# Block attention and a gated feed-forward on one core: first q by hardware queues, earlier data moves, a limit of three loads in flight, and new instruction orders

## The chip, the cores and the metric

The kernel runs on one core of one Trainium2 chip. The metric is device microseconds of one execution. "Span" is the length of the profiled execution on the core; the times stand about 1.8 us above it. Most executions of the kernel before lie within 0.5% of their median. A run more than 1.5% above the fastest of its kernel is called slow and is left out of ratios, but medians are of all runs. Where a profile is quoted it is of a fast run, unless the text says otherwise.

Engines as the profile names them: PE (TensorE matmuls), PEld (TensorE weight loads), DVE (VectorE), ACT (ScalarE), POOL (GpSimd), SP (SyncE); a q behind the name is that engine's queue or sequencer.

## The reference

```python
# q, k, v: (8 batches, 8 heads, 576 positions, 64), blocks of 64 positions
scores = q_block @ k_block.T / 8
attn   = exp(scores - max) / (sum + 1e-9)
x      = attn @ v_block                # 4608 tokens x 512 after the transpose of heads
h      = ((x @ w1) * (x @ w2)) @ w3    # d_ff = 1024
out    = h @ w_out                     # 4608 x 512
```

## The kernel before

The tokens are cut into 18 "pairs" of 256 tokens; two pairs are a group, which from pair 4 on shares one run through w1 and w2. w3 and w_out are multiplied once into one matrix (steps V, W, Z), so that each pair needs only one output product (O). A string gives the program order of all steps; each engine runs its own instructions in that order.

```python
# letter = step, number = pair; a few lines of the order
q0.0 k0.0 q0.1 k0.1 v0 q1.0 q1.1 k1.0 k1.1 i0 v1 q2 k2 i1 v2 i2 i3 q3 k3 v3 o h0 h1 q4 k4 v4
D0.0.32.64 T0.0.0 T0.1.0 T0.0.1 S0.0 T0.1.1 q5 k5 v5 E0.0 S0.1 E0.1 P0.0 P0.1 ...
# q k v i o h  loads by GpSimd, cast from f32 to bf16 on the way (i = quarter of w1 and w2)
# T  transpose of q or k on VectorE, in 32x32 blocks      S  scores   E  exp on ScalarE
# P  attention times v   N  normalise   X  transpose of x on VectorE
# G  SyncE moves of q and k, H  SyncE moves of x: from pair 8 on, into rows that allow 64x64 matmuls
# A B  x times w1, x times w2 into the halves of one PSUM tile
# C  copy of half A to SBUF (ScalarE)   M  C's copy times half B (VectorE)
# O Y Q  output product, copy, store   D  warm-up matmuls on zeros
# in profiles: s_ps is the PSUM tile of S, pv of P, ab_ps of A and B, w_ps of W, o_ps of O; a_sb is C's copy

def load(dst, src):
    return inorder(nc.gpsimd.dma_start(dst, src))

def do_P(p, hh=None):                   # ... cut
    if p < 8:      # 32-row blocks: 64 small matmuls a pair
        ...
    else:          # moved data: 32 matmuls of 64x64
        for g, r in ((0, 0), (1, 1), (1, 0), (0, 1)):
            mm(pv[half[g], r, m * W:(m + 1) * W], lhsT=e[half[r], u, 4 * g + m, :],
               rhs=vbuf[p % 6][half[r], u, 4 * g + m, 0:W], start=True, stop=True)

def do_C(p, j):
    a_t[p, j] = msb.tile([P, 512], f32, tag="a_sb", bufs=3, name="a_sb")
    inorder(nc.scalar.copy(a_t[p, j][:], ps_t[p, j][:, 0, :]))
```

q and k share five buffers, v has six: a load also waits until its buffer has been read.

The softmax here doesn't subtract the row's maximum and nothing guards it: scores larger than these inputs give would overflow.

Of the kernel before, what the change touches and what calls it, by code (L numbers as in the profile page):

```python
# [9 lines left out]
q0.0 k0.0 q0.1 k0.1 v0 q1.0 q1.1 k1.0 k1.1 i0 v1 q2 k2 i1 v2 i2 i3 q3 k3 v3 o h0 h1 q4 k4 v4  # L10
D0.0.32.64 T0.0.0 T0.1.0 T0.0.1 S0.0 T0.1.1 q5 k5 v5 E0.0 S0.1 E0.1 P0.0 P0.1 T1.0.0 N0.0 T1.1.0
T1.0.1 S1.0 T1.1.1 q6 k6 v6 E1.0 X0.0 S1.1 N0.1 X0.1 P1.0 E1.1 T2.0 A0.0 T2.1 q7 k7 B0.0 C0.0 P1.1
v7 M0.0 A0.1 N1.0 B0.1 C0.1 X1.0 S2 N1.1 E2 M0.1 X1.1 P2 A1.0 N2.0 B1.0 X2.0 C1.0 A1.1 N2.1 B1.1
M1.0 C1.1 X2.1 A2.0 M1.1 B2.0 C2.0 A2.1 M2.0 B2.1 T3.0 C2.1 A0.2 M2.1 B0.2 C0.2 T3.1 q8 k8 v8 A1.2
M0.2 B1.2 C1.2 S3 M1.2 A2.2 E3 B2.2 C2.2 P3 M2.2 A0.3 N3.0 B0.3 X3.0 C0.3 A1.3 N3.1 B1.3 M0.3 C1.3
X3.1 A2.3 M1.3 B2.3 C2.3 A3.0 M2.3 B3.0 V0 C3.0 A3.1 M3.0 B3.1 V1 C3.1 A3.2 M3.1 B3.2 C3.2 V2 A3.3
M3.2 B3.3 C3.3 V3 W0 M3.3 T4.0 W1 Z0 V4 V5 T4.1 q9 k9 v9 W2 Z1 V6 V7 T5.0 S4 Z2 W3 T5.1 q10 k10 E4
T6.0 T6.1 P4 v10 q11 k11 Z3 S5 N4.0 O0 E5 X4.0 N4.1 X4.1 T7.0 O1 T7.1 Y0 Q0 T8.0 P5 v11 q12 k12 Y1
S6 T8.1 O2 Q1 E6 N5.0 X5.0 N5.1 X5.1 O3 T9.0 T9.1 Y2 G4.0 P6 v12 q13 k13 A4.0 N6.0 B4.0 G4.1 Y3 X6.0
N6.1 C4.0 A4.1 X6.1 B4.1 C4.1 M4.0 Q2 S7 Q3 M4.1 A4.2 E7 T10.0 B4.2 C4.2 T10.1 P7 v13 q14 k14 A4.3  # L20
M4.2 B4.3 N7.0 C4.3 A4.4 X7.0 M4.3 B4.4 C4.4 N7.1 A4.5 M4.4 B4.5 C4.5 X7.1 S8 M4.5 S9 E8 A4.6 T11.0
# [23 lines left out]
def kernel(  # L45
# [11 lines left out]
    nc = tc.nc  # L57
    B, H, S, D = q.shape
# [36 lines left out]
    def load(dst, src):  # L95
        return inorder(nc.gpsimd.dma_start(dst, src))  # L96
# [14 lines left out]
    vbuf = [consts.tile([P, 2, H, VW], bf, name=f"vbuf{i}") for i in range(6)]  # L111
# [16 lines left out]
    HH = H // 2  # L128

# [51 lines left out]
    def do_G(g, a):  # L181
# [250 lines left out]
```

## Time and profile before

Time 251.4 us (median of 4 runs, 249.8 to 252.8); span 249.3 us.

| engine | busy us | share of the span |
|---|---|---|
| TensorE matmuls | 226.9 | 91% |
| VectorE | 154.5 | 62% |
| ScalarE | 83.4 | 33% |
| GpSimd (issuing loads) | 86.9 | 35% |

The prediction shows the lines that carry the reading. In the rows of digits there the span is cut into 40 equal slices, and each digit is the busy share of one in tenths (9 is 90% or more); in the row PEclk it is the TensorE clock that was granted. From the list of waits (engine, line, what it waited for, then total us, times, longest us): VectorE's transposes of q and k waited for q loads three times in all.

```profile
DVE qkT L177 <- DMA qk<-in_q_dram: 8.3, 3, 3.1
```

All three of those waits end by 20.2 us, and those for k by 22.4. After that the loads were always ahead of the transposes.

### The profile page before, as it was taken

The numbers are of one execution on the slowest core, as the hardware profiler recorded it, in microseconds if no ns is written. First come the engines' busy times: TensorE is split into PE (matmuls) and PEld (weight loads), VectorE is DVE, ScalarE is ACT, GpSimd is POOL, SyncE is SP. The second block draws the span as 40 slices with busy tenths as digits, with TensorE's granted clock in tenths as the row PEclk, the third lists the DMA queues.
The fourth block names the chain that finished last, engine by engine and source line by source line (L and its number), as shares of the span: only waits on it lengthen the run. The fifth ranks groups of instructions, "written<-read, shape, count | busy, mean of one in ns | idle before, by whom it ended". The sixth has DMA issues, their size and how long they took to land.

```text
span 249.3 us, 6372 instructions
## 1 busy us (share of the span) xinstructions
PE 226.9 (91%) x2740; PEld 122.0 (49%) x2760; DVE 154.5 (62%) x236; ACT 83.4 (33%) x116; POOL 86.9 (35%) x116
## 2 busy tenths in 40 slices
PE   3328899999999999999999999999999999999992
PEld 2225688874455445444444444444444444444441
DVE  2566965899879588999998798918440331233000
ACT  2110324332343333535335325262332332331322
POOL 8977854486997254573660000000000000000000
PEclk9999999999999999999999999999999999999998
DMA  7999999999999999999999974635502200400334
GB/s 67 145 165 182 193 185 201 196 174 172 155 169 209 221 225 249 177 209 193 204 194 235 271 128 99 147 76 199 151 3 84 84 0 9 162 0 1 139 116 168
DMA packets 93660, 37.12 MB, mean 149 GB/s; under 512 B 77120, under 2 KB 86592, under 8 KB 93632
## 3 DMA queue, kind: packets, MB, share of 16 engines
q0 software_dynamic: 84736, 19.41, 84.6%
q1 hardware_dynamic: 8896, 17.31, 24.0%
q8 instruction: 22, 0.36, 0.6%
q14 instruction: 6, 0.05, 0.1%
HBM read 38.80 MB, written 9.44 MB: 194 GB/s over the span
## 4 chain that ended last, share of the span: by engine, by line
PE 73%; DMA 17%; POOL 3%; DVE 2%; issue 1%; ACT 1%; SPq 0%; DVEq 0%; ACTq 0%; POOLq 0%
PE ab_ps L93 41%; PE o_ps L93 22%; DMA out_dram<-o_sb 6%; DMA w<-in_moe_w_dram 6%; PE w_ps L93 6%; DMA qkm<-qkT 5%; PE s_ps L93 3%; PE pv L93 2%; POOL qk L96 2%; DVE qkT L177 1%; POOL vbuf L96 1%; ACT e L209 0%; DVE ab L321 0%; POOL w L96 0%; ACT a_sb L306 0%
## 5 line engine op out<-in xcount | busy, mean ns | idle before, releaser
L93 PE MATMUL ab_ps<-xt,w 128*128 128x512 bf16 (+1 forms) x697 | 130.0, 343 | 1.1 <-DMA w<-in_moe_w_dram 0.5
L93 PEld LDWEIGHTS <-w 128*128 128x128 bf16 x704 | 67.8, 99 | 55.6 <-DMA w<-in_moe_w_dram 0.9
L321 DVE TENSOR_TENSOR ab<-a_sb,ab_ps 128x512 bf16<-128x512 f32 x72 | 48.9, 679 | 49.3 <-ACT a_sb L306 49.2
L306 ACT COPY a_sb<-ab_ps 128x512 f32<-128x512 f32 x72 | 42.2, 585 | 87.9 <-PE ab_ps L93 85.9
L93 PE MATMUL o_ps<-w3o,ab 128*128 128x512 bf16 (+1 forms) x285 | 63.3, 373 | 0.6
L177 DVE STREAM_TRANSPOSE qkT<-qk 128x1024 bf16<-128x1024 bf16 (+1 forms) x40 | 45.6, 1178 | 11.0 <-DMA qk<-in_q_dram 8.3
L93 PEld LDWEIGHTS <-ab 128*128 128x128 bf16 x296 | 28.5, 98 | 32.2
L96 POOL DMA_DIRECT2D vbuf<-in_v_dram x40 | 33.8, 854 | 14.6 <-DMA qk<-in_q_dram 6.4
L351 ACT COPY o_sb<-o_ps 128x1024 f32<-128x1024 f32 x17 | 17.2, 1012 | 42.8 <-PE o_ps L93 38.8
L239 DVE TENSOR_TENSOR xn<-pv,rc 128x512 bf16<-128x512 f32 x36 | 24.9, 692 | 1.2
L96 POOL DMA_DIRECT2D qk<-in_k_dram x26 | 20.2, 782 | 10.0 <-DMA vbuf<-in_v_dram 7.3
L96 POOL DMA_DIRECT2D qk<-in_q_dram x26 | 20.3, 788 | 8.2 <-DMA qk<-in_k_dram 2.3
L209 ACT ACTIVATE e<-s_ps 128x1024 bf16<-128x1024 f32 (+1 forms) x18 | 17.1, 978 | 8.9 <-PE s_ps L93 8.7
L93 PE MATMUL pv<-vbuf,e 64*32 64x65 bf16 (+1 forms) x832 | 11.0, 200 | 4.5 <-DMA vbuf<-in_v_dram 3.3
L93 PE MATMUL w_ps<-wo,w3T 128*128 128x512 bf16 x62 | 14.0, 379 | 0.1
L93 PEld LDWEIGHTS <-e 64*32 64x32 bf16 (+1 forms) x832 | 8.3, 99 | 11.5 <-issue 6.6
L236 DVE RECIPROCAL rc<-pv 128x8 f32<-128x8 f32 x36 | 6.9, 192 | 11.3 <-PE pv L93 11.2
L96 POOL DMA_DIRECT2D w<-in_moe_w_dram x16 | 11.1, 696 | 7.4 <-DMA wo<-in_moe_w_out_dram 3.4
L259 DVE STREAM_TRANSPOSE xm<-xn 128x512 bf16<-128x512 bf16 x20 | 13.6, 697 | 0.2
L251 DVE STREAM_TRANSPOSE xt<-xn 128x512 bf16<-128x512 bf16 x16 | 11.3, 707 | 0.4
L93 PEld LDWEIGHTS <-qkT 32*64 32x64 bf16 x512 | 5.8, 116 | 11.2 <-DVE qkT L177 9.2
L344 DVE COPY o_sb<-o_ps 128x256 f32<-128x256 f32 x1 | 0.4, 424 | 16.0 <-PE o_ps L93 16.0
(19 smaller groups left out, 45.4 us busy)
## 6 DMA issues: line engine op xcount, KB each, us to landing
out_dram<-o_sb SPq DMA_DIRECT2D x17, 512.0 KB, 2.9
qkm<-qkT SPq DMA_DIRECT2D x40, 128.0 KB, 7.2
vbuf<-in_v_dram POOLq DMA_DIRECT2D x32, 128.0 KB, 8.7
w<-in_moe_w_dram POOLq DMA_DIRECT2D x16, 256.0 KB, 10.0
qk<-in_q_dram POOLq DMA_DIRECT2D x10, 256.0 KB, 8.3
qk<-in_k_dram POOLq DMA_DIRECT2D x10, 256.0 KB, 10.1
xt<-xm SPq DMA_DIRECT2D x40, 64.0 KB, 3.0
qk<-in_q_dram POOLq DMA_DIRECT2D x8, 128.0 KB, 5.1
```

The source lines that it names most:

```text
L93: return inorder(nc.tensor.matmul(*a, **kw))
L96: return inorder(nc.gpsimd.dma_start(dst, src))
L177: inorder(nc.vector.transpose(qkT_t[g][:, :, p % 2, s, heads(h)].rearrange("p e h (y t) -> p h t e y", t=2), qk_t[p][:, s, heads(h)].rearr ...
L209: inorder(nc.scalar.activation(e_t[p][:, :, heads(hh)], s_t[p][:].rearrange("p u (h q) -> p u h q", q=CH)[:, :, heads(hh)], Exp, scale=sca ...
L236: inorder(nc.vector.reciprocal(rc[:], pv[:, :, :, D:W]))
L239: inorder(nc.vector.tensor_mul(xn_t[p][:, u], pv[:, :, :, 0:D], rc.to_broadcast([P, 2, 4, D])))
L251: inorder(nc.vector.transpose(new_xt(g)[:].rearrange("p (o t) -> p o t", o=KO)[:, :, t0:t0 + UT] .rearrange("p o (m y) -> p m o y", y=BL), ...
L259: inorder(nc.vector.transpose(xm_t[g][:, u, :, m].rearrange("p o (c y) -> p c o y", y=BL), xn_t[p][:].rearrange("p u r m d -> p (u r) m d" ...
L306: inorder(nc.scalar.copy(a_t[p, j][:], ps_t[p, j][:, 0, :]))
L321: inorder(nc.vector.tensor_mul(o, view(a_t.pop((p, j))[:]), view(ps_t.pop((p, j))[:, 1, :])))
L344: inorder(copy(o_sb[:, u, n0:n1], t[:, 0, 0:n1 - n0]))
L351: inorder(nc.scalar.copy(o_sb[:], ps_t.pop(p)[:]))
```

## The change

Its intent: start sooner, by taking the first q out of GpSimd's queue and by a better order of loads; give pairs 6 and 7 the cheaper 64x64 form of attention times v; and from pair 8 on keep the load queue short, so that the moves of q, k and x arrive sooner. The instruction orders were searched anew for all of it.

```diff
+    last = []
+    tick = consts.tile([P, 1], bf, name="tick")
-    def load(dst, src):
-        return inorder(nc.gpsimd.dma_start(dst, src))
+    def load(dst, src, paced=False):
+        if paced:                       # paced: p >= 8
+            inorder(nc.gpsimd.tensor_copy(tick[0:1], last[-3]))
+        ins = inorder(nc.gpsimd.dma_start(dst, src))
+        ...                             # last.append(one element of dst)
+        return ins
+    def do_R(h):                        # first q, half h, f32
+        raw_t[h] = msb.tile([P, HH, 2 * D], f32, tag="o_sb", name="raw")
+        inorder((nc.sync, nc.scalar)[h].dma_start(raw_t[h][:], q[0, heads(h), 0:4 * CH, :]...))
+    def do_K(h):
+        inorder(nc.scalar.copy(qk_t[0][:, 0, heads(h)], raw_t[h][:]))
     # do_P, do_X, do_AB, do_M: the moved form of x; do_G, do_H: other order of the moves (below)
-    if p < 8:
+    if p < 6:
-    vbuf ... range(6)     ab ... bufs=3
+    vbuf ... range(7)     ab ... bufs=4
 ORDER
-q0.0 k0.0 q0.1 k0.1 v0 q1.0 q1.1 k1.0 k1.1 i0 v1 q2 k2 i1 v2 i2 i3 q3 k3 v3 o h0 h1 q4 k4 v4
+R0 R1 k0 v0 q1 k1 v1 i1 i0 q2 k2 v2 i2 i3 q3 k3 v3 h0 o h1 q4 k4 v4 K0 K1 T0.0 T0.1 q5 k5 v5 S0 E0
 ...                                    # nearly all of the rest is new too
```

The one-element copy reads what the load three back has written. GpSimd therefore stands still until that load has landed: at most three loads are in flight.

Two things are cut from the diff. do_D makes its warm-up matmuls in another form. do_G and do_H issue their moves in another order, and the first four moves of x of a group now need only the first transpose of each of its pairs; before, each four needed both.

More of the change, by code (lines that the diff above doesn't have):

```diff
@@ L9 @@
 ORDER = """
-q0.0 k0.0 q0.1 k0.1 v0 q1.0 q1.1 k1.0 k1.1 i0 v1 q2 k2 i1 v2 i2 i3 q3 k3 v3 o h0 h1 q4 k4 v4
-D0.0.32.64 T0.0.0 T0.1.0 T0.0.1 S0.0 T0.1.1 q5 k5 v5 E0.0 S0.1 E0.1 P0.0 P0.1 T1.0.0 N0.0 T1.1.0
-T1.0.1 S1.0 T1.1.1 q6 k6 v6 E1.0 X0.0 S1.1 N0.1 X0.1 P1.0 E1.1 T2.0 A0.0 T2.1 q7 k7 B0.0 C0.0 P1.1
-v7 M0.0 A0.1 N1.0 B0.1 C0.1 X1.0 S2 N1.1 E2 M0.1 X1.1 P2 A1.0 N2.0 B1.0 X2.0 C1.0 A1.1 N2.1 B1.1
-M1.0 C1.1 X2.1 A2.0 M1.1 B2.0 C2.0 A2.1 M2.0 B2.1 T3.0 C2.1 A0.2 M2.1 B0.2 C0.2 T3.1 q8 k8 v8 A1.2
@@ L15 @@
-M0.2 B1.2 C1.2 S3 M1.2 A2.2 E3 B2.2 C2.2 P3 M2.2 A0.3 N3.0 B0.3 X3.0 C0.3 A1.3 N3.1 B1.3 M0.3 C1.3
-X3.1 A2.3 M1.3 B2.3 C2.3 A3.0 M2.3 B3.0 V0 C3.0 A3.1 M3.0 B3.1 V1 C3.1 A3.2 M3.1 B3.2 C3.2 V2 A3.3
-M3.2 B3.3 C3.3 V3 W0 M3.3 T4.0 W1 Z0 V4 V5 T4.1 q9 k9 v9 W2 Z1 V6 V7 T5.0 S4 Z2 W3 T5.1 q10 k10 E4
-T6.0 T6.1 P4 v10 q11 k11 Z3 S5 N4.0 O0 E5 X4.0 N4.1 X4.1 T7.0 O1 T7.1 Y0 Q0 T8.0 P5 v11 q12 k12 Y1
-S6 T8.1 O2 Q1 E6 N5.0 X5.0 N5.1 X5.1 O3 T9.0 T9.1 Y2 G4.0 P6 v12 q13 k13 A4.0 N6.0 B4.0 G4.1 Y3 X6.0
@@ L20 @@
-N6.1 C4.0 A4.1 X6.1 B4.1 C4.1 M4.0 Q2 S7 Q3 M4.1 A4.2 E7 T10.0 B4.2 C4.2 T10.1 P7 v13 q14 k14 A4.3
-M4.2 B4.3 N7.0 C4.3 A4.4 X7.0 M4.3 B4.4 C4.4 N7.1 A4.5 M4.4 B4.5 C4.5 X7.1 S8 M4.5 S9 E8 A4.6 T11.0
-B4.6 E9 T11.1 P8 v14 q15 k15 C4.6 A4.7 M4.6 G5.0 B4.7 C4.7 N8.0 A6.0 M4.7 B6.0 N8.1 C6.0 G5.1 A6.1
-X8.0 B6.1 M6.0 C6.1 X8.1 P9 v15 q16 k16 A6.2 M6.1 N9.0 B6.2 C6.2 N9.1 A6.3 M6.2 B6.3 C6.3 X9.0 A6.4
-M6.3 B6.4 C6.4 X9.1 A6.5 T12.0 H4.0 B6.5 C6.5 M6.4 A6.6 M6.5 B6.6 T12.1 H4.1 C6.6 S10 S11 M6.6 E10
@@ L25 @@
-A6.7 T13.0 B6.7 E11 P10 v16 q17 k17 T13.1 C6.7 O4 M6.7 G6.0 N10.0 N10.1 X10.0 G6.1 P11 v17 Y4 X10.1
-O5 N11.0 N11.1 Q4 X11.0 X11.1 T14.0 A8.0 H5.0 Y5 B8.0 T14.1 C8.0 A8.1 M8.0 B8.1 H5.1 C8.1 T15.0 A8.2
-B8.2 M8.1 C8.2 T15.1 Q5 A8.3 B8.3 C8.3 M8.2 G7.0 S12 M8.3 S13 E12 A8.4 T16.0 B8.4 E13 G7.1 P12 T16.1
-C8.4 A8.5 B8.5 M8.4 C8.5 N12.0 A8.6 M8.5 B8.6 C8.6 N12.1 A8.7 M8.6 B8.7 C8.7 X12.0 P13 M8.7 A10.0
-X12.1 B10.0 C10.0 N13.0 A10.1 M10.0 B10.1 N13.1 C10.1 A10.2 X13.0 B10.2 M10.1 C10.2 X13.1 S14 S15
@@ L30 @@
-M10.2 E14 A10.3 H6.0 T17.0 B10.3 E15 P14 T17.1 C10.3 A10.4 H6.1 M10.3 B10.4 C10.4 N14.0 A10.5 M10.4
-B10.5 G8.0 C10.5 N14.1 A10.6 M10.5 B10.6 C10.6 X14.0 P15 G8.1 X14.1 A10.7 M10.6 B10.7 N15.0 C10.7 O6
-N15.1 M10.7 X15.0 X15.1 H7.0 S16 Y6 S17 O7 E16 E17 H7.1 P16 Y7 O8 Q6 N16.0 Q7 N16.1 X16.0 X16.1 P17
-Y8 A12.0 N17.0 Q8 B12.0 N17.1 C12.0 A12.1 X17.0 B12.1 M12.0 C12.1 X17.1 A12.2 M12.1 H8.0 B12.2 C12.2
-A12.3 M12.2 B12.3 C12.3 H8.1 A12.4 M12.3 B12.4 C12.4 A12.5 M12.4 B12.5 C12.5 A12.6 M12.5 B12.6 C12.6
@@ L35 @@
-A12.7 M12.6 B12.7 C12.7 O9 M12.7 O10 Y9 Q9 A14.0 Y10 B14.0 C14.0 Q10 A14.1 M14.0 B14.1 C14.1 A14.2
-M14.1 B14.2 C14.2 A14.3 M14.2 B14.3 C14.3 A14.4 M14.3 B14.4 C14.4 A14.5 M14.4 B14.5 C14.5 A14.6
-M14.5 B14.6 C14.6 A14.7 M14.6 B14.7 C14.7 O11 M14.7 O12 Y11 Q11 A16.0 Y12 B16.0 C16.0 Q12 A16.1
-M16.0 B16.1 C16.1 A16.2 M16.1 B16.2 C16.2 A16.3 M16.2 B16.3 C16.3 A16.4 M16.3 B16.4 C16.4 A16.5
-M16.4 B16.5 C16.5 A16.6 M16.5 B16.6 C16.6 A16.7 M16.6 B16.7 C16.7 O13 M16.7 O14 Y13 Q13 O15 Y14 Q14
-O16 Y15 Q15 O17 Y16 Q16 Y17 Q17
+R0 R1 k0 v0 q1 k1 v1 i1 i0 q2 k2 v2 i2 i3 q3 k3 v3 h0 o h1 q4 k4 v4 K0 K1 T0.0 T0.1 q5 k5 v5 S0 E0
@@ new lines @@
+T1.0 D2.0.0.1 P0 N0.0 T1.1 q6 k6 v6 X0.0 S1 N0.1 E1 X0.1 P1 A0.0 N1.0 N1.1 A0.1 X1.0 X1.1 B0.1 T2.0
+C0.1 A1.0 T2.1 q7 k7 v7 B0.0 C1.0 C0.0 M0.1 S2 M0.0 B1.0 E2 A0.2 M1.0 B0.2 C0.2 P2 M0.2 A1.1 N2.0
+A0.3 X2.0 B1.1 N2.1 C0.3 C1.1 A1.2 T3.0 B0.3 C1.2 X2.1 A1.3 M1.1 B1.3 M0.3 B1.2 T3.1 q8 k8 v8 C1.3
+A2.0 M1.2 S3 C2.0 M1.3 B2.0 E3 A2.1 M2.0 V0 P3 C2.1 B2.1 N3.0 A2.2 M2.1 B2.2 X3.0 C2.2 N3.1 A2.3
+B2.3 X3.1 M2.2 A3.0 V2 B3.0 C3.0 V3 A3.1 B3.1 C3.1 M3.0 C2.3 W1 V1 M2.3 W0 V6 V7 M3.1 T4.0 A3.2 Z0
+W3 T4.1 q9 k9 v9 C3.2 Z1 V4 V5 S4 Z3 T5.0 B3.2 E4 W2 M3.2 T5.1 q10 k10 v10 T6.0 T6.1 q11 k11 P4 v11
@@ new lines @@
+Z2 A3.3 N4.0 O0 N4.1 T7.0 X4.0 T7.1 q12 k12 S5 B3.3 E5 O1 C3.3 T8.0 Y0 M3.3 Q0 T8.1 P5 v12 q13 k13
+X4.1 Y1 O2 N5.0 Q1 X5.0 N5.1 X5.1 T9.0 S6 Y2 A4.0 T9.1 A4.1 C4.0 E6 B4.0 G4.0 B4.1 C4.1 M4.0 P6 v13
+q14 k14 M4.1 S7 Q2 N6.0 A4.2 E7 G4.1 N6.1 B4.2 C4.2 X6.0 P7 v14 A4.6 M4.2 X6.1 B4.6 C4.6 N7.0 A4.5
+N7.1 A4.3 X7.0 B4.3 C4.3 M4.6 H3.0 C4.5 B4.5 X7.1 A4.4 M4.3 M4.5 B4.4 C4.4 H3.1 T10.0 S8 A4.7 T10.1
+q15 k15 B4.7 C4.7 E8 O3 T11.0 M4.7 M4.4 T11.1 P8 v15 q16 k16 Y3 A6.0 G5.0 N8.0 B6.0 N8.1 C6.0 S9
@@ new lines @@
+M6.0 A6.5 G5.1 X8.0 A6.1 C6.5 T12.0 E9 B6.5 B6.1 C6.1 M6.5 P9 v16 M6.1 A6.2 X8.1 B6.2 C6.2 N9.0 A6.3
+N9.1 B6.3 C6.3 X9.0 A6.6 M6.3 H4.0 B6.6 M6.2 C6.6 X9.1 A6.4 M6.6 S10 H4.1 C6.4 S11 T12.1 q17 k17
+B6.4 E10 A6.7 E11 M6.4 B6.7 T13.0 C6.7 O4 M6.7 T13.1 T14.0 G6.0 P11 Y4 A8.2 N11.0 B8.2 N11.1 Q3 C8.2
+G6.1 A8.3 M8.2 P10 v17 C8.3 B8.3 N10.0 O5 N10.1 M8.3 X10.0 X10.1 X11.0 A8.1 T14.1 H5.0 A8.0 X11.1
+B8.0 C8.0 C8.1 B8.1 M8.0 H5.1 Y5 A8.6 T15.0 B8.6 C8.6 M8.1 A8.4 M8.6 Q4 B8.4 T15.1 C8.4 S12 S13 M8.4
@@ new lines @@
+E12 G7.0 A8.5 T16.0 B8.5 E13 A8.7 C8.5 G7.1 P12 M8.5 C8.7 B8.7 N12.0 A10.2 M8.7 B10.2 N12.1 C10.2
+A10.5 M10.2 B10.5 X12.0 C10.5 P13 M10.5 A10.0 N13.0 A10.3 C10.0 N13.1 B10.0 C10.3 X12.1 S14 M10.0
+S15 E14 B10.3 A10.6 E15 M10.3 B10.6 X13.0 C10.6 P15 H6.0 M10.6 A10.4 X13.1 B10.4 C10.4 O6 M10.4 Q5
+H6.1 N15.0 N15.1 T16.1 P14 Y6 A10.1 N14.0 B10.1 N14.1 C10.1 A10.7 T17.0 B10.7 C10.7 A12.1 M10.7
+A12.7 M10.1 C12.1 T17.1 B12.1 C12.7 A12.3 X14.0 G8.0 A12.0 M12.1 X14.1 B12.7 C12.0 C12.3 B12.0 M12.7
+G8.1 A12.2 M12.0 B12.2 X15.0 C12.2 X15.1 B12.3 H7.0 M12.2 O7 M12.3 H7.1 A12.6 Q6 A12.4 C12.6 A12.5
@@ new lines @@
+C12.4 B12.6 C12.5 Y7 B12.4 M12.6 B12.5 Q7 M12.4 A14.0 M12.5 B14.0 C14.0 S16 M14.0 S17 E16 A14.5
+B14.5 E17 A14.6 C14.5 P16 M14.5 C14.6 B14.6 N16.0 O8 N16.1 M14.6 P17 Y8 A14.3 N17.0 B14.3 Q8 N17.1
+C14.3 O9 M14.3 X16.0 A14.1 Y9 A14.2 C14.1 Q9 B14.1 O10 M14.1 X16.1 X17.0 X17.1 H8.0 B14.2 Y10 O11
+H8.1 Q10 O12 Y11 C14.2 Q11 M14.2 A16.4 Y12 B16.4 C16.4 Q12 A14.4 M16.4 A16.2 C14.4 A16.7 B14.4 B16.2
+M14.4 A16.6 B16.6 C16.6 C16.2 A16.1 C16.7 M16.2 B16.7 B16.1 M16.7 A14.7 M16.6 A16.5 C16.1 M16.1
+A16.3 C16.5 C14.7 B16.5 C16.3 B14.7 M16.5 O13 M14.7 A16.0 B16.0 C16.0 Y13 B16.3 M16.0 O14 Q13 M16.3
@@ L41 @@
+O15 Y14 Q14 O16 Y15 Q15 Y16 Q16 O17
 """
@@ L93, in mm @@
         return inorder(nc.tensor.matmul(*a, **kw))
-    def load(dst, src):
-        return inorder(nc.gpsimd.dma_start(dst, src))
+    last = []
[4 more added lines that the diff above has]
+        ins = inorder(nc.gpsimd.dma_start(dst, src))
+        d = dst[0:1]
+        while len(d.shape) > 2:
+            d = d[:, 0]
+        last.append(d[:, 0:1])
+        return ins
     def psum(name):
@@ L110 @@
     inorder(nc.vector.memset(zero[:], 0.0))
-    vbuf = [consts.tile([P, 2, H, VW], bf, name=f"vbuf{i}") for i in range(6)]
+    vbuf = [consts.tile([P, 2, H, VW], bf, name=f"vbuf{i}") for i in range(7)]
     for t in vbuf:
@@ L128 @@
     HH = H // 2
+    raw_t = {}
+    def do_R(h):
+        raw_t[h] = msb.tile([P, HH, 2 * D], f32, tag="o_sb", name="raw")
+        inorder((nc.sync, nc.scalar)[h].dma_start(
+            raw_t[h][:], q[0, heads(h), 0:4 * CH, :].rearrange("h (p t) d -> p h (t d)", t=2)))
+    def do_K(h):
+        if 0 not in qk_t:
+            qk_t[0] = io.tile([P, 2, H, 2 * D], bf, tag="qk", bufs=5, name="qk")
+        inorder(nc.scalar.copy(qk_t[0][:, 0, heads(h)], raw_t[h][:]))
     def heads(h):
@@ L138, in load_qk @@
                 load(qk_t[p][at * BL:(at + m) * BL, s, heads(h)],
-                     (q, k)[s][b, heads(h), c * CH:(c + m) * CH, :].rearrange("h (p t) d -> p h (t d)", t=2))
+                     (q, k)[s][b, heads(h), c * CH:(c + m) * CH, :].rearrange("h (p t) d -> p h (t d)", t=2),
+                     p >= 8)
     def load_v(p):
@@ L143, in load_v @@
             for at, b, c, m in spans(4 * p + 2 * u, 2):
-                load(vbuf[p % 6][at * CH:(at + m) * CH, u, :, 0:D],
-                     v[b, :, c * CH:(c + m) * CH, :].rearrange("h p d -> p h d"))
+                load(vbuf[p % 7][at * CH:(at + m) * CH, u, :, 0:D],
+                     v[b, :, c * CH:(c + m) * CH, :].rearrange("h p d -> p h d"), p >= 8)
     def load_w(dst, ap, n0, n1):
@@ L184, in do_G @@
             qkm_t[g] = asb.tile([P, 2, 2, 2, H, CH], bf, tag="qkm", bufs=2, name="qkm")
-        for i in (2 * a, 2 * a + 1):
-            for e in range(2):
-                move(qkm_t[g][blk[2 * a + e], i % 2], qkT_t[g][blk[i], e])
+        for i in (0, 2, 1, 3):
+            e = (i + a) % 2
+            move(qkm_t[g][blk[i // 2 * 2 + e], i % 2], qkT_t[g][blk[i], e])
     def do_S(p, hh=None):
@@ L226, in do_P @@
                                lhsT=e[half[r], u, 2 * g + m % 2, m // 2 * BL:(m // 2 + 1) * BL],
-                               rhs=vbuf[p % 6][half[r], u, 2 * g + m % 2, 0:W], start=True, stop=True)
+                               rhs=vbuf[p % 7][half[r], u, 2 * g + m % 2, 0:W], start=True, stop=True)
                 else:
@@ L230, in do_P @@
                         mm(pv[half[g], r, m * W:(m + 1) * W], lhsT=e[half[r], u, 4 * g + m, :],
-                           rhs=vbuf[p % 6][half[r], u, 4 * g + m, 0:W], start=True, stop=True)
+                           rhs=vbuf[p % 7][half[r], u, 4 * g + m, 0:W], start=True, stop=True)
     def do_N(p, u):
@@ L248, in do_X @@
         g, m = divmod(p, 2)
-        if p < 8:
+        if p < 6:
             t0 = m * PT + u * UT
@@ L266, in do_H, with do_D @@
         xt = new_xt(g)[:].rearrange("p (s c) -> p s c", s=2)
-        for k_ in range(2):
-            for i in (2 * a, 2 * a + 1):
-                move(xt[blk[2 * a + k_], i % 2], xm_t[g][blk[i], k_].rearrange("p o m t -> p (o m t)"))
+        for i in (0, 2, 1, 3):
+            move(xt[blk[i // 2 * 2 + a], i % 2], xm_t[g][blk[i], a].rearrange("p o m t -> p (o m t)"))
     ab_t, ps_t, a_t, o_t = {}, {}, {}, {}
-    def do_D(which, p, n, cols):
-        d, key = (s_t, p) if which == 0 else (ps_t, (p, 0))
+    def do_D(which, p, j, n):
+        d, key = ((s_t, p), (ps_t, (p, j)), (pv_t, (p, 0)))[which]
         if key not in d:
@@ L278, in do_D @@
         for _ in range(n):
-            mm(d[key][:, 0, 0:cols], lhsT=zero[:, 0:P], rhs=zero[:, 0:cols], start=True, stop=True)
+            mm(d[key][:, 0, :], lhsT=zero[:, 0:P], rhs=zero[:], start=True, stop=True)
     def do_AB(p, j, f, which):
-        if p >= 8:
+        if p >= 6:
             rhs = new_xt(p // 2)[:].rearrange("p (s o t) -> p o s t", s=2, o=KO)
@@ L310, in do_M @@
         if g not in ab_t:
-            ab_t[g] = msb.tile([P, FO, GT], bf, tag="ab", bufs=3, name="ab")
+            ab_t[g] = msb.tile([P, FO, GT], bf, tag="ab", bufs=4, name="ab")
         if p < 4:
@@ L314, in do_M @@
             view = lambda t: t.rearrange("p (j t) -> p j t", j=2)
-        elif p < 8:
+        elif p < 6:
             o = ab_t[g][:, j]
@@ L390, in load_half3 @@
         load_w3(i * n, (i + 1) * n)
-    do = {"q": load_q, "k": load_k, "v": load_v, "i": load_w12, "o": load_wo, "h": load_half3, "T": do_T, "S": do_S, "E": do_E, "G": do_G, "H": do_H,
+    do = {"q": load_q, "k": load_k, "v": load_v, "i": load_w12, "o": load_wo, "h": load_half3, "T": do_T, "S": do_S, "R": do_R, "K": do_K, "E": do_E, "G": do_G, "H": do_H,
           "P": do_P, "N": do_N, "X": do_X, "A": do_A, "B": do_B, "C": do_C, "M": do_M, "D": do_D, "V": do_V,
```

## The prediction

> **What bounds the kernel now.** I read the page first (busy shares and the slices), then the chain that ended last in order of time, then the timeline of TensorE alone, and last the waits.
>
> The page, parts 1 and 2:
>
> ```profile
> PE 226.9 (91%) x2740; PEld 122.0 (49%) x2760; DVE 154.5 (62%) x236; ACT 83.4 (33%) x116; POOL 86.9 (35%) x116
> ...
> PE   3328899999999999999999999999999999999992
> ...
> DMA  7999999999999999999999974635502200400334
> ```
>
> TensorE is below nine tenths in the first five slices (6.2 us each) and in the last; from about 31 us on it is full. The transfer engines are full for the first 22 slices, about 137 us. So the kernel is a start-up bound by arriving data, then a long stretch bound by matmuls. The chain says the same; its first and last pieces:
>
> ```profile
> 9.09 0.63 POOL w L96
> 9.72 7.24 DMA w<-in_moe_w_dram
> 16.96 0.28 issue
> 17.24 7.36 DMA w<-in_moe_w_dram
> 24.61 0.05 issue
> 24.65 1.05 PE ab_ps L93 x8
> ...
> 213.21 13.81 PE ab_ps L93 x64
> ```
>
> Two weight loads in a row, each over 7 us from issue to landing, lie on the path until 24.6 us; from there it is almost all TensorE. A run of 64 matmuls of 512 columns takes 13.81 us, 215.8 ns each. The timeline of TensorE (start, length, line, operation, count, idle before) shows the holes:
>
> ```profile
> 14.44 0.64 PE L93 MATMUL s_ps<-qkT 32*64 32x64 bf16 x32 [3.22 <-DVE qkT L177]
> ...
> 19.48 3.28 PE L93 MATMUL ab_ps<-xt,w 128*128 128x256 bf16 x16
> ...
> 28.18 11.10 PE L93 MATMUL ab_ps<-xt,w 128*128 128x256 bf16 x96
> ...
> 42.33 12.40 PE L93 MATMUL ab_ps<-xt,w 128*128 128x256 bf16 x112
> ...
> 101.94 5.35 PE L93 MATMUL ab_ps<-xt,w 128*128 128x512 bf16 x23
> 107.23 0.45 PE L93 MATMUL pv<-vbuf,e 64*64 64x65 bf16 x32
> ...
> 148.96 0.93 PE L93 MATMUL s_ps<-qkm 64*64 64x64 bf16 x63 [0.41 <-DMA qkm<-qkT]
> ```
>
> **Budget of TensorE.** From the program's counts and these rows: 256 matmuls of 256 columns for pairs 0 to 3 at 110 ns (12.33 us for 112 in the chain) = 28.2; 448 of 512 columns for the other pairs at 215.8 ns = 96.7; the fused weight product 64 x 215.8 = 13.8; the output 280 x 215.8 ns + 16 x 110 ns = 62.2; scores 8 x 0.64 + 10 x 0.32 = 8.3; attention times v 8 x 0.63 + 10 x 0.38 = 8.8. Sum 218.0 us. The span is 249.3, so 31.3 us are not work. By 28.18 us only 32 small weight matmuls (3.5) and scores and pv of three pairs (3.8) are done, 7.3 us: 20.9 us lost at the start. The last matmul ends at 244.3: 5.0 us of last copy, store and end. From 28.18 to 244.3 are 216.1 us for 210.7 of work: 5.4 us lost in the whole middle. Therefore nearly everything there is to win is in the start.
>
> **What the Trainium skill says.**
> "DMA: Bandwidth & Descriptors", Issuing engines are not separate DMA queues: issuing from several engines shares the same 16 engines and saves only the issuer's time. The trace shows how large that is here: a load of half a q tile holds GpSimd 0.77 us for 128 KB, 170 GB/s at most, and the first 10 us moved a mean of 92 GB/s against about 180 later. So early on the issuer is a limit, which the new queues relieve; later they could not.
> The same page, Rules for kernel authors: a cast during a transfer is issued from GpSimd. Hence the raw tile and two casting copies for q by the hardware queues. The trace agrees as far as it goes: all casting loads are GpSimd's, all SyncE transfers keep their type.
> "TensorE: Matmul & The Clock Gate", Part 1: after idling, the array runs at half rate until some 3.4 us of activity. It agrees: the first 16 weight matmuls took 3.28 us, 205 ns each, the 112 later ones 111 ns. The new kernel pays this too.
> "TensorEngine Tiling (Array Packing)", Key Properties: changing the tiling mode drains the array. About 0.1 us at each change fits: 24 x 215.8 ns after 101.94 ends at 107.12, and the next row starts at 107.23. Some 40 such changes make up most of the 5.4 us in the middle.
>
> **The change part by part.**
> 1. First q. The kernel before issues q and k of pair 0 as four halves on GpSimd, 0.78 us each, about 3.1 us. Now k is one load (about 0.89) and q goes by SyncE and ScalarE. GpSimd is 2.2 us further on at v of pair 0. Added: two ScalarE casts of 128x512 at 585 ns (the copy row of that size), 1.2 us on an engine that has nothing to do then. The 32 warm-up matmuls become one.
> 2. Order of loads. Before: pair 0, q and k of 1, weight quarter 0, v of 1, q and k of 2, quarter 1. Now: pairs 0 and 1 whole, quarters 1 and 0, then pair 2. Issue times from GpSimd's rows: 1.24 + k 0.88 + v 1.78 + q, k 1.76 + v 1.78 + quarter 1 1.5 = 8.9 us for the first matrix of quarter 0, the time at which it was issued before too (8.99), but with 0.5 MB more of weights issued ahead of it. By bytes: up to it 2.05 MB; q outside GpSimd's queue costs about 0.25 more (it reads the same), some 0.15 overlaps: 2.45 MB at the 165 to 170 GB/s of 10 to 20 us, from 3 us on, lands at 17.5 to 18. The first weight matmul thus starts near 17.7 instead of 19.5. What counts is what follows: both quarters and both pairs are then there, so A and B of two pairs run on. Five groups of eight (4.3 us warm, about 6 with the half clock) last until 23.8. Pair 2's k is at 3.2 MB, 21.8 us, plus a 1.3 us transpose: 23.1, in time. After scores of pair 2 at 24.4 us, 7.55 us of work are done, against 7.3 at 28.18: **4.0 us won**, an estimate good to about 2 us.
> 3. x of pairs 6 and 7 by transfers. Attention times v takes 32 matmuls of 64x64 in 0.38 us in place of 64 in 0.63: 2 x 0.25 = **0.5 us** on the bound engine. The transposes on VectorE are the same in number and size. Added are eight transfers on SyncE (0.59 us of issue each, 3 us to landing in the median), ahead of the weight stage of pair 6. The q and k moves start at pair 8 as before.
> 4. Three loads in flight from pair 8 on. A one-element copy on GpSimd waits for the load three back. Loads to landing now stand at 8 to 19 us between 78 and 130 us, the q and k moves at 7.2, the x moves at 6 to 7 there but 3.0 in the median with the queue empty. Shorter queues should take the moves to 3 or 4 us. What this can gain is what TensorE waits for moves: 0.7 us on matmuls and 0.5 on weight loads, with slow first matmuls about 1.5 us. I count **0.7**.
> 5. Orders. The late scores move further back among weight matmuls, spreading VectorE's work, which was 90% busy up to 160 us and 25% after 180. This gains only where TensorE waited, nearly nowhere. The tail keeps three or four output groups, the last copy and store: 0.
>
> Sum 4.0 + 0.5 + 0.7 = 5.2 us; with a little for the 0.7 us of waits for x at 31.7 us, about 6. The span should be 243.3; the times stand 1.9 above the span (251.2 to 249.3), so **245.2 us**, 2.4% less.
>
> **The rivals.**
> Arrivals decide alone. If the first 30 us are bound by bytes, another order only changes which data comes when, and the gain shrinks to the 1.5 us that q takes in the queue (0.25 MB at 170 GB/s). For it: the transfer engines are full from the second slice. Against it: the mean of 92 GB/s in the first 10 us, and matmuls at 19.48 that waited for v of pair 1 by order, not for their weights. It would give 248 to 249.
> The pacing becomes the new wait. 48 loads remain from pair 8 on; at 4.5 us to landing (3.8 to 4.4 in the empty queue of the first 5 us) three in flight make 0.67 a microsecond, 72 us. Begun near 66 us, the last is issued near 138, where it was 129. Pairs 12, 14 and 15 then land only about 4 us before their transposes, by my count along the new order. At 5.5 us each they would be late and VectorE, in program order, would stall with its products behind it: 3 to 6 us lost, 248 to 251.
> The x moves of pair 6 are late. The last four follow the transpose of pair 7 by about 6 us of TensorE work, with 2.4 us of issue and 3 to 7 of landing: up to 3 us lost once, 248.
> Better: the half clock ends earlier and stores no longer delay moves: 242.
>
> **Range and chances.** The start alone spans 2 to 6 us, the middle between +2 and -4. I take 241.5 to 249.5, centre 245.2. The 2% line is at 246.2, one microsecond above the centre. Faster 0.60, same 0.37, slower 0.03: to be slower all loads would have to be late by several microseconds.
>
> **What would show it.** Right: the first weight matmul at 17 to 19 us, TensorE unbroken from about 24; start loss 16 to 18 us in place of 20.9; pv of pairs 6 and 7 in 0.38 us each; moves of q and k below 5 us to landing; no wait for a load over 1 us after 60 us. Wrong: new holes on TensorE between 85 and 150 us released by VectorE's transposes or by x moves, or a start that still lasts to 27 us, with waits for weights or for k of pair 2.

## The result, and the profile after

The changed kernel takes 268.25 us (median of 4 runs, 266.3 to 269.8). Its fast runs against those of the kernel before stand at 1.0668, with a 95% interval of 1.0573 to 1.0764. Ratios here are the mean time of one kernel's fast runs over that of the other's of the same rounds, so not quite the ratio of the medians. The forecast was 245.2; the time is outside its range.

The page after, parts 1 and 2:

```profile
PE 229.6 (86%) x2645; PEld 120.4 (45%) x2665; DVE 152.5 (57%) x233; ACT 82.5 (31%) x116; POOL 91.2 (34%) x159
...
PE   0269998999996968949988949999999999989995
...
PEclk9999999999999999967999977999999999999999
DMA  9999999999999998999999999941750225300244
```

The start is better (the third slice of 40 has 6 where it had 2), but from the 13th to the 24th slice, 80 to 160 us, TensorE has holes, where before it was full. The granted clock falls with two of them. The transfer engines stay full until about 173 us, before until about 143, though the kernel reads and writes the same 38.8 and 9.4 MB of HBM.

TensorE alone in order of time:

```profile
17.98 5.74 PE L92 MATMUL ab_ps<-xt,w 128*128 128x256 bf16 x40 [0.63 <-DMA w<-in_moe_w_dram]
23.65 0.71 PE L92 MATMUL s_ps<-qkT 32*64 32x64 bf16 x64
...
28.22 8.03 PE L92 MATMUL ab_ps<-xt,w 128*128 128x256 bf16 x72
...
84.00 0.45 PE L92 MATMUL pv<-vbuf,e 64*64 64x65 bf16 x32
87.06 0.70 PE L92 MATMUL s_ps<-qkT 32*64 32x64 bf16 x64 [2.61 <-DVE ab L344]
...
117.58 8.80 PE L92 MATMUL ab_ps<-xt,w 128*128 128x512 bf16 x28 [3.79 <-DVE ab L344]
...
158.92 6.03 PE L92 MATMUL ab_ps<-xt,w 128*128 128x512 bf16 x16 [3.52 <-DVE ab L344]
```

The first weight matmul comes at 17.98, and by 28.22 us the kernel has done 10.8 us of work where the one before had 7.3 at 28.18: 3.5 us won. (The 10.8: scores and pv of three pairs 3.8, and 64 matmuls of 256 columns at 110 ns, 7.0.) At 66.9 us, the first output product, 2.1 us of that are left, counted the same way: before, that product began at 70.5 us with 1.5 us more work done ahead of it (scores of one pair more, 0.6, and eight matmuls, 0.9).

Then the holes. Those above name a product on VectorE as their end. That is not the cause: VectorE works in program order, and its own list of waits says what held it.

```profile
DVE qkT L200 <- DMA qk<-in_q_dram: 25.2, 8, 5.3
```

25.2 us of waiting for q loads, three times what it was, and 21.8 us of it after 70 us, in six waits. The products stood behind those transposes. The chain that ended last shows where the loads waited in turn (start, length, what):

```profile
88.94 11.46 DMA vbuf<-in_v_dram
100.41 0.02 issue
100.43 0.02 POOLq L100
100.45 0.08 issue
100.53 0.18 POOL tick L100
100.71 0.32 issue
101.02 0.49 POOL qk L101
...
152.02 4.96 DMA qk<-in_q_dram
156.99 0.02 issue
157.01 1.31 DVE qkT L200
```

A load lands, the one-element copy (tick) runs, the next load is issued, it lands, and so on from 84 to 157 us. There are eleven such landings on the chain, 63.6 us together, 5.8 us each; from a landing to the next issue go another 0.6 us (100.41 to 101.02). The view of the tile tick gives the whole length (count, durations in ns, first and last start):

```profile
L100 POOL COPY tick<-qk x26: 176/176/180, 67.8 to 166.0; 1x1 bf16<-1x1 bf16 x26
L100 POOL COPY tick<-vbuf x22: 176/176/177, 69.1 to 164.4; 1x1 bf16<-1x1 bf16 x22
```

48 loads in 98.2 us, 0.49 a microsecond: with three in flight a load's turn is 6.1 us (98.2 / 48 x 3). The trace kept the landing of 42 of the 48; they took 5.5 us from issue in the mean, and 5.5 and 0.6 make the 6.1. In the kernel before the last load was issued at 128 us.

**Where the 17.6 us of span went.** Holes of TensorE between 80 and 160 us sum to 16.2 us (2.6, 1.2, 1.4, 1.2, 0.2, 3.8, 0.6, 0.3, 1.2, 0.3, 3.5), and later ones to 1.1. Not all of them are the loads': 2.9 us of the 16.2 end with a ScalarE copy (e6 and e12 take these up), and two holes, 2.0 us, are put down to moves of x. The kernel before had 1.9 us after 80 us (holes 1.2, slow first scores 0.7). After the holes of 3.8 and 3.5 us the matmuls ran slowly: 28 in 8.80 and 16 in 6.03 us, where 215.8 ns each would be 6.04 and 3.45; another 5.3 us. Less 2.1 won at the start and 0.5 by pairs 6 and 7 that makes 18.1, within a microsecond of the difference of the spans.

### The profile page after: what moved, and what is told of

It reads as the page before. It is cut to its first block, busy times and chain, and to the rows that moved or that the text cites. A ratio compares the mean times of both kernels' runs of the same rounds, so it can differ in the third digit from the quotient of the medians.

```text
span 266.9 us, 6269 instructions
## 1 busy us (share of the span) xinstructions
PE 229.6 (86%) x2645; PEld 120.4 (45%) x2665; DVE 152.5 (57%) x233; ACT 82.5 (31%) x116; POOL 91.2 (34%) x159
## 4 chain that ended last, share of the span: by engine, by line
PE 52%; DMA 34%; POOL 6%; issue 3%; DVE 3%; ACT 1%; POOLq 0%; DVEq 0%
PE ab_ps L92 25%; PE o_ps L92 19%; DMA vbuf<-in_v_dram 17%; DMA w<-in_moe_w_dram 10%; PE w_ps L92 5%; DMA qk<-in_q_dram 5%; DMA qk<-in_k_dram 2%; POOL qk L101 2%; POOL w L101 2%; POOL vbuf L101 1%; PE s_ps L92 1%; ACT a_sb L329 1%; PE pv L92 1%; POOL tick L100 1%; DVE ab L344 1%
## 5 line engine op out<-in xcount | busy, mean ns | idle before, releaser
L92 PE MATMUL ab_ps<-xt,w 128*128 128x512 bf16 (+1 forms) x700 | 137.8, 351 | 14.3 <-DVE ab L344 7.5
L200 DVE STREAM_TRANSPOSE qkT<-qk 128x1024 bf16<-128x1024 bf16 x36 | 46.3, 1300 | 29.5 <-DMA qk<-in_q_dram 25.2
L101 POOL DMA_DIRECT2D vbuf<-in_v_dram x40 | 33.6, 844 | 10.2 <-issue 3.5
L233 ACT ACTIVATE e<-s_ps 128x1024 bf16<-128x1024 f32 x18 | 18.0, 1027 | 17.3 <-PE s_ps L92 17.1
L101 POOL DMA_DIRECT2D qk<-in_q_dram x23 | 17.9, 777 | 8.1 <-issue 2.1
L101 POOL DMA_DIRECT2D qk<-in_k_dram x24 | 18.8, 783 | 3.5 <-issue 1.1
L92 PE MATMUL s_ps<-qkT 32*64 32x64 bf16 x512 | 6.4, 204 | 13.8 <-DVE qkT L200 11.2
L283 DVE STREAM_TRANSPOSE xm<-xn 128x512 bf16<-128x512 bf16 x24 | 16.2, 693 | 0.1
L100 POOL COPY tick<-qk 1x1 bf16<-1x1 bf16 x26 | 4.6, 176 | 29.4 <-DMA qk<-in_q_dram 18.0
L92 PE MATMUL pv<-vbuf,e 64*64 64x65 bf16 (+1 forms) x736 | 9.6, 200 | 2.5 <-DVE ab L344 1.2
L385 DVE STREAM_TRANSPOSE w3T<-w 128x1024 bf16<-128x1024 bf16 x8 | 9.6, 1224 | 1.9 <-DMA w<-in_moe_w_dram 1.4
## 6 DMA issues: line engine op xcount, KB each, us to landing
wo<-in_moe_w_out_dram POOLq DMA_DIRECT2D x4, 256.0 KB, 10.2
```

The lines of the kernel that those rows point to most:

```text
L92: return inorder(nc.tensor.matmul(*a, **kw))
L100: inorder(nc.gpsimd.tensor_copy(tick[0:1], last[-3]))
L101: ins = inorder(nc.gpsimd.dma_start(dst, src))
L200: inorder(nc.vector.transpose(qkT_t[g][:, :, p % 2, s, heads(h)].rearrange("p e h (y t) -> p h t e y", t=2), qk_t[p][:, s, heads(h)].rearr ...
L233: inorder(nc.scalar.activation(e_t[p][:, :, heads(hh)], s_t[p][:].rearrange("p u (h q) -> p u h q", q=CH)[:, :, heads(hh)], Exp, scale=sca ...
L283: inorder(nc.vector.transpose(xm_t[g][:, u, :, m].rearrange("p o (c y) -> p c o y", y=BL), xn_t[p][:].rearrange("p u r m d -> p (u r) m d" ...
```

## The experiments

**Theory P:** the limit of three loads in flight is the cause; the data arrive too slowly, VectorE stalls in order, TensorE behind it, and loses its clock as well. **Rival O:** the new orders, with transposes earlier and scores later, make the holes by themselves. Each group of four kernels ran on one chip with runs of the kernel before beside it: 251.5 (e1 to e4), 251.3 (e5 to e8) and 250.9 us (e9 to e12). All results were correct.

### e1: the changed kernel without the limit

```diff
-        if paced:
+        if False and paced:
```

> The changed kernel with the waits of the loads taken out, nothing else. Theory P (the limit of three loads in flight costs the time): VectorE's 25 us of waits for q loads go, TensorE has no holes between 80 and 160 us, and what remains is the 2 us that the start has won by 67 us and 0.5 us of the x moves: 247 to 250 us, at or a little below the kernel before. Rival O (the new order of the operations, with transposes moved earlier and scores later, makes the holes by itself): it stays above 260 us with the same holes released by the products on VectorE.

252.8 us, ratio 1.0084 (1.0034 to 1.0134). The waits of VectorE for q loads are gone:

```profile
DVE qkT L200 <- DMA qk<-in_q_dram: 2.5, 2, 1.9
```

Theory P holds and rival O falls as the cause of the loss. But the time is 2.8 us above the 247 to 250 expected, and the kernel is not faster than before, as it should have been by my steps; e6 takes that up.

### e2: six loads in flight

```diff
-            inorder(nc.gpsimd.tensor_copy(tick[0:1], last[-3]))
+            inorder(nc.gpsimd.tensor_copy(tick[0:1], last[-6]))
```

> The changed kernel with six loads in flight instead of three. Theory P: loads arrive at most twice as fast as with three (0.49 a microsecond measured there), and then TensorE's need of about 5.5 loads in 10 to 12 us sets the pace again: within 2 us of the kernel with no limit, 247 to 252 us. Rival O: above 260 us as with three.

250.7 us, ratio 0.9981 (0.9946 to 1.0017). The ticks run from 62.7 to 130.0 us, so the last load goes out about when it did before. The whole loss hung on the number three.

"No limit" is not quite the word for e1 and for the kernel before. Their loads signal their landings on eight semaphores in turn, and GpSimd waits before it uses one again. In the trace of e10 (below), which kept every landing, no load is issued before the load eight back has landed; many follow it by 0.28 us. So the change went from eight in flight to three.

### e3: the kernel before with three loads in flight

The same `load`, `last` and `tick` put into the kernel before, `paced` for pairs from 8 on; its order unchanged.

> The kernel before with one thing added: three loads in flight from pair 8 on, its own orders. Theory P: the 48 loads take about 97 us as in the changed kernel instead of some 66, the last is issued near 160 us instead of 129, and the time rises by 8 to 17 us, to 259 to 268. Rival O: the old order hides it, within 2 us of the kernel before.

279.6 us, ratio 1.1102 (1.1007 to 1.1197): 28 us slower, beyond even theory P's range. The ticks need the same time, 99 us:

```profile
L100 POOL COPY tick<-qk x26: 176/176/179, 69.1 to 168.3; 1x1 bf16<-1x1 bf16 x26
```

So the pace belongs to the limit, not to the order. The old order pays 28 us for it (VectorE waits 21.9 us for q and 16.7 for k), the changed kernel 17. The changed kernel softens the limit; its order does not cause the loss. How much of the 11 us is the order and how much the added buffers (seven for v, four for the products) was not tested.

### e4: the kernel before with only the first q changed

```diff
-q0.0 k0.0 q0.1 k0.1 v0 ...
+R0 R1 k0.0 k0.1 v0 ...
-D0.0.32.64 T0.0.0 ...
+D0.0.32.64 K0 K1 T0.0.0 ...
```

> The kernel before with one thing changed: q of pair 0 by the two hardware queues, with the two casts on ScalarE, its own order otherwise. Theory: GpSimd saves two issues of 0.78 us, loads behind are up to 1.5 us earlier, the chain through two weight loads that ends at 24.6 us moves by as much: 249.5 to 251 us, 0.5 to 1.5 us less than before. Rival (arrivals are bound by bytes even in the first 10 us): no change, within 0.4 us.

249.75 us, ratio 0.9939 (0.9911 to 0.9966): 1.7 us by the medians, 1.5 by the ratio, against 1.56 us that two issues of 0.78 us take. The fused weight product starts at 52.88 us instead of 54.57. This part does what it was meant to do. (Two loads fewer in GpSimd's queue also free two of the eight places; the two effects were not separated.)

### e5: four loads in flight

`last[-4]` in place of `last[-3]`.

> The changed kernel with four loads in flight. Theory P: one load in 6.1 us divided by the number in flight; three gave 0.49 a microsecond and 97 us for 48 loads, six gave 250.7 us. Four give 0.66 a microsecond at the same time per load, 73 us for 48 loads, the last issued near 141 us: some stalls stay, 252 to 257 us. If loads slow down in proportion when more are in flight (engines already full with three), four would be no better than three: 262 to 268.

Fast runs 252.4 and 253.8 us (two slow ones 256.2 and 259.4, median of all four 255.0). The ticks run from 66.7 to 147.7, 81 us; a load's turn, 81 / 48 x 4, is now 6.75 us instead of 6.1. Loads slow down somewhat when more are in flight, but far from in proportion: the mean landing of the paced loads that the traces kept is 5.5 us with three, 6.4 with four, 7.6 with six and 10.2 in e1. Against the number in flight:

| in flight | time, us | first to last tick, us |
|---|---|---|
| 3 | 268.25 | 98 |
| 4 | 252.4, 253.8 | 81 |
| 6 | 250.7 | 67 |
| not paced (eight) | 252.8 | no ticks; first to last issue 65 |

From three to four most of the loss is gone. That fits a supply that falls just below need.

### e6: six in flight, and copies behind half B

With six in flight TensorE's own list of waits has this at its head after the start-up:

```profile
PE ab_ps L92 <- ACT a_sb L329: 4.0, 6, 1.2
```

In 29 places the new order has the copy C of half A ahead of the matmuls B that fill the other half of the same PSUM tile; the order before has none. The traces show what that adds: 34 matmuls of A and B carry a wait for ScalarE with the new order, 6 after the edit, 15 in the kernel before. The edit puts each such C right behind its B:

```diff
-... X7.0 B4.3 C4.3 M4.6 H3.0 C4.5 B4.5 X7.1 ...
+... X7.0 B4.3 C4.3 M4.6 H3.0 B4.5 C4.5 X7.1 ...
 # and 28 more
```

> Six in flight, and in the order every ScalarE copy of half A is put behind the matmuls of half B of the same tile (29 places where the new order has it ahead). Theory C: where the copy stands ahead, the matmuls of B wait for it, 4.0 us in six waits with six in flight; these go, and the product needs both halves anyway: 246 to 248.5 us. Rival (the product on VectorE, not the copy, holds the tile, and the wait only moves to it): 250 to 251.5, no change.

Fast runs 247.1 and 245.9 us, ratio 0.9814 (0.9776 to 0.9852); two more runs, 250.4 and 251.8, count as slow. The wait is gone from the list, which after 50 us has five entries, of 0.2 to 0.5 us; three of them:

```profile
PE ab_ps L63 <- DMA xt<-xm: 0.5, 1, 0.5
PE ab_ps L63 <- DVE ab L315: 0.3, 2, 0.2
PE w_ps L63 <- ACT w3o L369: 0.2, 1, 0.2
```

(The order stands on one line in this file, hence the other line numbers.) The new orders did have a cost of their own, which the larger one hid. Its size is less sure than its sign: by the ratios it is 4.2 us here (e2 to e6), 2.3 when the same program was run again (e2 to e9) and 2.4 without the limit (e1 to e10).

### e7: three in flight, q and k of pairs 8 to 11 not moved

```diff
 # do_S
-            if p < 8:
+            if p < 12:
 ORDER: without G4.0 G4.1 G5.0 G5.1
```

> The changed kernel (three in flight), but q and k of pairs 8 to 11 are not moved: their scores take 64 small matmuls instead of 32 (4 x 0.32 us = 1.3 us more on TensorE). Theory M (a load takes 6 us and not 4.5 because moves and stores share the 16 engines): the loads land sooner between 85 and 115 us, 3 to 5 us in place of 6 to 9, and the time falls by 3 to 7 us in spite of the 1.3: 262 to 266 us. Rival (the 6 us are the load's own): 268 to 270 us.

261.7 us (median of all four), ratio 1.0321 (1.0240 to 1.0402; fast runs 257.6 and 260.9), a little below the 262 to 266 expected. The ticks take 91.5 us instead of 98.2. Issues to landing in the window 108 to 120 us (output, input, queue, count, KB each, median us), first in the changed kernel, where eight moves of q and k ran in that window:

```profile
vbuf<-in_v_dram POOLq DMA_DIRECT2D x3, 128.0 KB, 6.7
qk<-in_q_dram POOLq DMA_DIRECT2D x1, 256.0 KB, 6.5
qk<-in_k_dram POOLq DMA_DIRECT2D x1, 256.0 KB, 9.1
```

and here, without them (this profile is of a run of the slow state, so only the landings are used; the q and k loads are also the smaller ones of another pair, so v is the fair comparison):

```profile
vbuf<-in_v_dram POOLq DMA_DIRECT2D x4, 128.0 KB, 4.9
qk<-in_q_dram POOLq DMA_DIRECT2D x2, 128.0 KB, 3.9
qk<-in_k_dram POOLq DMA_DIRECT2D x2, 128.0 KB, 4.0
```

The loads land later beside the moves, v in 6.7 us instead of 4.9. Three and four loads are few; of all paced loads issued from 85 to 115 us, where the moves are missing here, 12 took 5.9 us in the mean with them and 15 took 4.3 without, while over 80 to 160 us the medians of v are 5.6 and 5.3. So part of the slow pace is what the moves take from the loads, and the limit then turns each longer landing into a lower rate. The edit also frees the scores of pairs 8 to 11 from waiting for moves; how much of the time won is that was not separated.

### e8: the kernel before with x moved from pair 6 on

Thresholds 8 to 6 as in the diff; X6.0 and X7.0 put behind the second normalisation, H3.0 and H3.1 behind X7.1.

> The kernel before with x of pairs 6 and 7 moved by transfers (32 matmuls of 64x64 in place of 64 for each pair), its own order with the two transposes put behind the second normalisation and the eight moves behind the last transpose. Theory: 0.5 us less TensorE work and no new wait: 250.4 to 251.2 us. Rival: the moves are late for the weight stage of pair 6 by up to 3 us: 252 to 254 us.

257.2 us, ratio 1.0242 (1.0219 to 1.0265): slower by 5.8. TensorE's timeline, the first weight matmuls of pair 6:

```profile
108.62 6.47 PE L93 MATMUL ab_ps<-xt,w 128*128 128x512 bf16 x16 [6.14 <-DMA qkm<-qkT]
```

A hole of 6.1 us, then 16 matmuls in 6.47 us instead of 3.45. The eight moves of x were issued from 97.3 to 102.3 us and landed 6.7 us later in the median; the q and k moves named as the end of the hole were issued right behind. That name is wrong: these matmuls read x, the eighth move of x landed at 108.32, 0.3 us before they start, and the first q and k move whose landing the trace kept landed at 112.55. The rival's mechanism is right, at twice the size given. But this is a harder case than the changed kernel's: the old do_H lets none of the eight moves go before X7.1, the new one sends four after X7.0.

### e9, e10, e11: what the best version owes to what

e9 is the program of e6 again; e10 is e9 without any limit; e11 is e9 with x moved from pair 8 on (thresholds back to 8, no H3.0 and H3.1).

> The same program as in e6, in more rounds, as its four times there stood 6 us apart (245.9 to 251.8). Theory C: 246 to 249 us, ratio to the kernel before 0.980 to 0.988, clear of it. Rival (the two low times were luck): ratio 0.99 or above.

> As e9 but with no limit on the loads. If a limit is worth something by itself (shorter queues for the moves), this is 1 to 3 us slower than e9, as e1 was 2.1 slower than e2: 249 to 251 us. If only the waits of half B were in the way, it equals e9 within 0.7 us.

> As e9 but with x moved from pair 8 on, as in the kernel before. TensorE does 0.5 us more (pv of pairs 6 and 7 in 0.63 instead of 0.38 us), and 16 moves fewer wait in SyncE's queue. Theory: the new order leaves the moves time, so they gain their 0.5 us: this is 0.3 to 0.7 us slower than e9. Rival: the waits for x moves in e6 (0.5 us) cost as much as they save: equal or faster.

| | median us | ratio to before | 95% interval |
|---|---|---|---|
| e9 | 249.2 | 0.9889 | 0.9844 to 0.9934 |
| e10 | 250.6 | 0.9988 | 0.9946 to 1.0030 |
| e11 | 250.6 | 0.9995 | 0.9961 to 1.0028 |

e9 is faster than the kernel before by about 1% on fast runs, and faster than the changed kernel by some 7%. It spreads more than the others: of its ten runs in e6 and e9 four are slow, the longest at 255.0 us. Its ratio lies between the two expectations, 0.980 to 0.988 and 0.99 or above, and above e6's, so neither is confirmed. On fast runs the gain is 1 to 2%; the mean of all ten runs is 249.5 us, 0.7% less than the kernel before. With the limit of six it is 1.0% faster than without (e10 over e9 0.9988 / 0.9889), as e2 was than e1, so a limit seems to help a little once it does not starve the transposes. That rests on leaving out e9's two slow runs: with them the means are 250.0 and 250.8 us.

The 0.5 us expected of the x moves came out as 2.7 us on fast runs (e11), 1.0 on all. e11's trace has a hole within the pv matmuls of pair 7 that the profile puts down to nothing (issue) and that e9's trace has not:

```profile
90.43 0.61 PE L63 MATMUL pv<-vbuf,e 64*32 64x65 bf16 x47 [2.97 <-issue]
```

Whether that hole belongs to the unmoved form of x was not tested; the size of this part stays open. e9's trace in turn has a hole that e11's has not, before the first weight matmuls of pair 6:

```profile
103.03 1.89 PE L63 MATMUL ab_ps<-xt,w 128*128 128x512 bf16 x8 [3.14 <-DMA qkm<-qkT]
```

The eighth move of x landed at 102.54. In e10's trace the same hole is 2.39 us, and the move landed at 103.50, 0.46 us before its end; in e6's it is 0.47. So the moves of x of pair 6 can be late in the new order too.

### e12: three in flight, copies behind half B

> The changed kernel with three in flight as it was, only the 29 copies put behind half B. Theory P: between 80 and 160 us loads set the pace, so a wait of TensorE that goes there wins nothing; only what lies outside that stretch, about 1.5 us, is won: 265 to 268 us. Rival (the waits of half B are a cause of their own beside the loads, and add up): 264 or less.

266.25 us, ratio 1.0560 (1.0501 to 1.0618). Between 1.0668 for the changed kernel and this lie some 2.7 us, with overlapping intervals. With three in flight the loads still set the pace; VectorE still waits 23.5 us for q loads. But 2.7 us is about what the same edit wins with eight in flight (2.4, e1 to e10), so that the two costs simply add up is not excluded.

## Why the prediction was wrong

**The start: right.** "The first weight matmul thus starts near 17.7 instead of 19.5": 17.98. "Five groups of eight ... last until 23.8": the next work begins at 23.65. "4.0 us won": 3.5 at 28 us (4.0 in e2's trace, the same program up to the first tick). When the output products begin 2.1 are left in the changed kernel, and 3.6, 2.0 and 2.9 in the traces of e2, e6 and e9. e4 shows the q part alone at 1.5 to 1.7 us; what the order of the loads adds was not run alone. And the gain does not reach the end by itself: e10, with neither the limit nor the early copies, is no faster than the kernel before (0.9988). The hole of 2.4 us before pair 6 is one loss that its trace shows; the rest stays open.

**pv of pairs 6 and 7: the duration right.** The run of 32 for pair 6 takes 0.45 us to its last end, the same row as for the pairs from 8 on before, from which the prediction's 0.38 us was taken. But the rival "The x moves of pair 6 are late ... up to 3 us lost once" came true in part: 0.5 to 3.1 us in the traces of e6, e10 and e9, more than the 0.5 us saved in two of them, and 6.1 us in the old order (e8).

**The pacing: the failed step.** Step 4 counted a gain of 0.7 us; the limit cost 15 to 18 us (e1 and e2 against the changed kernel). The rival "The pacing becomes the new wait" was given 3 to 6 us and little weight in the chances. Its mechanism was exactly what happened; its terms were mis-sized:
- "at 4.5 us to landing (3.8 to 4.4 in the empty queue of the first 5 us) three in flight make 0.67 a microsecond, 72 us". Measured: 0.49 a microsecond, 98 us. The turn of a load was 6.1 us: 5.5 to landing, and a hand-over of 0.6 from landing to the next issue that was left out. The 4.5 came from the first 5 us, with no moves or stores beside the loads; e7 shows that the moves lengthen them.
- I had written that "at 5.5 us each they would be late", and 5.5 is what they took. With a margin of 4 us over 70 and a landing time taken from the first 5 us, this rival should have had far more weight.
- "3 to 6 us lost" left out what a hole costs afterwards: 5.3 us after the two longest, where the granted clock is recorded as one half from 116.0 to 122.9 us and from 157.0 to 163.8. I cited that very behaviour and applied it to the start only.

**What the limit could gain was small, as step 4 said; what it takes was not in step 4.** Moves of q and k land in 5.6 us in the median instead of 7.2, not in "3 or 4", and without the limit the new order has them at 6.2 already (e1). The gain worth having was a microsecond or two, as six in flight suggests, the risk 17 us.

**The orders: wrong by a few microseconds.** Step 5 gave them 0. They lost 2 to 4 us by copies ahead of half B (e1 to e10, e2 to e6 and e9). The new order's lines showed it before any run: C ahead of B in 29 places, in none before. On the other side they absorbed, together with the added buffers, 11 us of the limit (e3 against the changed kernel). Step 5's shares were read a little high: VectorE was 81% busy up to 160 us and 21% after 180; nothing hung on them.

**Against the signs I had listed:** "new holes on TensorE between 85 and 150 us released by VectorE's transposes" was named as what would show it wrong, and that is what the trace shows.

## What to carry to other kernels

A limit on transfers in flight is a rate: number in flight over the time of one turn. Take that time from a loaded stretch of the trace, add the hand-over, look for the limit that the program has already (eight here), and compare the rate with the need before asking what shorter queues would gain; if the margin is smaller than the doubt in that time, the limit is the likeliest new bound. An engine that works in program order passes a late load on to everything behind it, and the holes of 3.5 and 3.8 us on TensorE were paid twice here, in the wait and in the slow matmuls behind it. That is no threshold: holes of 2.8 us in e3 and 3.0 in e11 were followed by half clock too, one of 3.1 in e9 was not. When an order comes from a search, test it again without the part it was searched with.

## What the Trainium skill lacked or had wrong

- "DMA: Bandwidth & Descriptors", Anatomy of one DMA: from its fit of 2.0 us plus bytes over 436 GB/s an estimate of 2.6 us comes out for the 0.26 MB that a v load of 128 KB in bf16 reads. Here the first such load took 4.4 us, with the four before it still in flight; in the median they took 5.4 us with three in flight (12 loads, 84 to 157 us) and 11.6 us with eight (8 loads, 84 to 120 us in the kernel before). The page has no landing time for a load beside the other loads, moves and stores of its core, which is what a limit on loads has to be sized by.
- "TensorE: Matmul & The Clock Gate", Back-to-back issue gap: it gives about 131 ns per matmul of 512 columns as sustained and calls the 216 ns of its formula an over-count. Here runs of 64 such matmuls with a weight load each took 13.81 us, 215.8 ns apiece. The formula fits and the sustained figure does not. What the page says in Part 1 of idling, half clock after an idle window of about 3.4 us, held: after idle gaps of 3.5 and 3.8 us the next 16 and 28 matmuls took 377 and 314 ns each. But a gap shorter than that window was enough in e3 (2.8 us, then a granted clock of 0.50 from 108.1 to 111.4 us).
- No page that I read tells what it costs to hold an issue back for an earlier load: 0.6 us from landing to the next issue here, with a one-element copy of 0.18 us in it, and 0.28 us where the load itself waits (e10).
